# Routing attention and an ELU layer on one core: masking of three batches moved from TensorE to VectorE

## The chip, the cores and the metric

The kernel runs on one core of a Trainium2 chip. A core has five engines that work side by side, each through its own queue in order: TensorE (PE in the profile, its weight loads PEld), VectorE (DVE), ScalarE (ACT), GpSimd (POOL) and SyncE (SP), which issues the transfers. The metric is the device time of a run in microseconds.

## The reference

Inputs are q, k, v of shape (4, 8, 768, 64), that is batch, heads, sequence, head dimension; 16 centroids per head; and two weight matrices of 512x2048 and 2048x512.

```python
q_assign = argmax(q_n @ c_n.T)          # per head, 16 clusters; the same for k
mask = q_assign[:, :, :, None] == k_assign[:, :, None, :]
scores = where(mask, q @ k.T / 8, -1e9)
attn = softmax(scores)
x = (attn @ v)  ->  (3072, 512)         # heads side by side
h = x @ w_in
out = where(h > 0, h, exp(min(h, 0)) - 1) @ w_out
```

A query attends only to the keys of its own cluster. That mask is what the change is about.

## The kernel before

**Blocks.** Attention is done in 48 blocks: 4 batches x 3 thirds of the queries (256 each) x 4 pairs of heads. One block is one iteration n of the main loop. Scores are held transposed: keys on the 128 partitions, queries along the free dimension. A block has six key tiles; two of them with two heads make a unit of 128 x 1024 numbers, which fills one of three PSUM buffers called `banks` (two 2 KB banks each). So there are three units per block.

**The mask before.** `assign` makes a one-hot matrix `hot` (cluster by token, bf16): L370 finds the largest similarity, L374 compares with it, L384 transposes. Because a pair of heads must lie on either half of the partitions, a second copy with the halves swapped is made (L388 on ScalarE in batch 1, L390 on VectorE later). `masks` (L401, ScalarE, two instructions per block) turns the queries' part into `qm`, which is 0 for the token's own cluster and -2^80 for the others. In `scores`, `plain` (L425) multiplies queries and keys, a pair of matmuls of 64 rows each per key tile, and `mask` (L437) adds `hot` times `qm` into the same bank, again a pair. The exponential (L448, ScalarE) of a masked score is then exactly 0.

**Values.** `values(n)` multiplies the exponentials `p` with v into `o_bank` (L506) and sums them over the keys by a matmul with ones (L495) into a `banks` buffer. From block 10 on, VectorE first adds the three units (`sums`, L483 to L485), so that four matmul records instead of 24 are left of the row sums. ScalarE takes the logarithm of the sum (L524), copies it to `e` (L525; `e` shares its buffer with `sim`, which `assign` reads), copies `o_bank` (L526) and makes 1/sum (L527); L528 and L529 on VectorE refine it; L532 on GpSimd multiplies it into `xT`.

**The ELU layer.** For each third, with a lag of seven blocks, four groups of steps lie in the iterations, one group each:
- n mod 4 = 3: `hidden` 0 and 1. Each is 16 matmuls into one `banks` buffer (L547), then exp on ScalarE (L557), a clamp on GpSimd (L558) and, after the next hidden step was issued, `elu` on VectorE (L564, L566 or L568), which releases the buffer.
- n mod 4 = 0: `hidden` 2 and 3.
- n mod 4 = 1: products `first` to `fourth` (L577), into o_bank, f_bank, o_bank, f_bank in turn. ScalarE evicts o_bank (L608, L619), VectorE f_bank (L614, L624); between them VectorE adds operands for later products (L609, L615).
- n mod 4 = 2: products `fifth` to `seventh`, into f_bank, o_bank, f_bank. VectorE evicts (L630, L637, L645); GpSimd adds (L638, L639); two stores follow.

The seven products are a Strassen-like form of the second matmul.

**The order of an iteration** is written out by hand: `values(n-1)`, loads, `scores(n)`, `masks(n+1)`, `sums(n)`, then in the last four iterations of a batch two 32x32-block transposes of the next batch's q and k on VectorE (`turn`, L319), then the group of the ELU layer. In a batch's last iteration, between the two hidden steps and after them, stand the similarities of the next batch (`similar`: matmuls L353 in two halves, each into a `banks` buffer that VectorE's transpose L360 releases) and `assign`. The first nine iterations also unpack the weights on VectorE and ScalarE (L249 to L274) and add weights (L304 to L307, with L305 on GpSimd).

**The check.** Near the end `verdict` adds up evidence that the fast path was valid (L676 to L686 on VectorE), sums it over the partitions by a small matmul (L688) and writes a flag. A second path runs only if it fails.

Buffers of a pool are given out again in the order in which they were released; a matmul into a buffer waits until its last reader has finished.

Of the kernel before, what the change touches and what calls it, by code (L numbers as in the profile page):

```python
# [9 lines left out]
F32 = mybir.dt.float32  # L10
BF16 = mybir.dt.bfloat16
U32 = mybir.dt.uint32
I32 = mybir.dt.int32
Act = mybir.ActivationFunctionType
Alu = mybir.AluOpType
# [3 lines left out]
P = 128  # L19
# [41 lines left out]
def main_path(ctx, tc, c, q, k, v, centroids, moe_w_in, moe_w_out, out):  # L61
# [7 lines left out]
    NQ = 3  # L69
# [24 lines left out]
    def banks():  # L94
        return short.tile([P, 2, 512], F32, name="banks", tag="banks")
# [66 lines left out]
    for e in range(2):  # L162
        rows = slice(64 * e, 64 * e + 64)
        nc.vector.tensor_reduce(
            big[rows],
            ident[rows].rearrange("q (h x e c) -> q x e h c", h=2, x=2, e=2)[:, :, e],
            axis=Axis.XY,
            op=Alu.add,
        )
    minus = const.tile([P, 2], F32, name="minus")  # L170
    nc.vector.tensor_scalar(minus, big, -BIG, None, op0=Alu.mult)
    nc.vector.tensor_scalar(big, big, BIG, None, op0=Alu.mult)
# [22 lines left out]
    cT = const.tile([P, P], F32, name="cT")  # L195
    nc.vector.tensor_copy(cT, cps[:, :P])

    count = const.tile([P, 4 * B + 1], F32, name="count")
    counted = {}
    r_sum = const.tile([P, NQ * len(pairs)], F32, name="r_sum")  # L200
# [108 lines left out]

    T, sim, hot, qm = {}, {}, {}, {}
    name_of = "qk"

    def turn(i, j):
# [45 lines left out]

    def assign(b, j, at, size):
        if at == 0:
            hot[b, j] = route.tile([P, 2, S], BF16, name="hot", tag=f"hot{j}", bufs=1 + j)
        cols = slice(at, at + size)
        n = size // NC
        s = sim[b, j][:, cols].rearrange("p (n c) -> p n c", c=NC)
        top = route.tile([P, HS // NC], F32, name="top", tag="top", bufs=1)[:, :n]
        oh = route.tile([P, HS], BF16, name="oh", tag="oh", bufs=1)[:, :size]
        nc.vector.tensor_reduce(top, s, axis=Axis.X, op=Alu.max)  # L370
        at = counted.setdefault(size, [])
        at.append(len(at) + (0 if size == HS else 4 * B - 2))
        at = at[-1]
        nc.vector.scalar_tensor_tensor(  # L374
            oh.rearrange("p (n c) -> p n c", c=NC),
            s,
            1.0,
            top.unsqueeze(2).to_broadcast([P, n, NC]),
            op0=Alu.mult,
            op1=Alu.is_equal,  # L380
            accum_out=count[:, at : at + 1],
        )
        h = hot[b, j]
        nc.vector.transpose(h[:, 0, cols], oh)  # L384
        for e in range(2):
            at = 64 * e
            if b == 0:
                nc.scalar.copy(h[64 - at : 128 - at, 1, cols], h[at : at + 64, 0, cols])  # L388
            else:
                nc.vector.tensor_copy(h[64 - at : 128 - at, 1, cols], h[at : at + 64, 0, cols])  # L390

    def side(pr, e):
        return int(pr // 2 != e)

    def masks(n):
        b, third, pr = blocks[n]
        qm[n] = route.tile([P, QS], BF16, name="qm", tag="qm", bufs=2)
        for e in range(2):
            rows = slice(64 * e, 64 * e + 64)
            m = big[rows, pr % 2 : pr % 2 + 1]  # L400
            nc.scalar.activation(  # L401
                qm[n][rows],
                hot[b, 0][rows, side(pr, e), ts(third, QS)],
                Act.Identity,
                scale=m,
                bias=minus[rows, pr % 2 : pr % 2 + 1],
            )
# [9 lines left out]
    def scores(n):  # L417
        b, third, pr = blocks[n]
        i = b * NPR + pr
        cols = ts(third, QS)  # L420

        def plain(s, kt):
            for e in range(2):
                rows = slice(64 * e, 64 * e + 64)
                nc.tensor.matmul(  # L425
                    s[:, e, ts(kt % 2, QS)],
                    lhsT=T[i, 1][rows, ts(kt, P)],
                    rhs=T[i, 0][rows, cols],
                    start=n > 0 or kt % 2 == 0,
                    stop=False,  # L430
                    skip_group_check=n == 0,
                )

        def mask(s, kt):
            for e in range(2):
                rows = slice(64 * e, 64 * e + 64)
                nc.tensor.matmul(  # L437
                    s[:, e, ts(kt % 2, QS)],
                    lhsT=hot[b, 1][rows, side(pr, e), ts(kt, P)],
                    rhs=qm[n][rows],  # L440
                    start=False,
                    stop=True,
                    skip_group_check=n == 0,
                )

        def exponentials(s, u):
            p = pu[n, u] = probs.tile([P, 2, 2 * QS], F32, name="p", tag="p")
            nc.scalar.activation(p, s, Act.Exp, scale=SCALE)  # L448

        if n == 0:  # L450

            turn_first = similar(0, 1, 0, QS)
            turn_rest = similar(0, 1, QS, 2 * QS)
            units = [banks() for _ in range(2)]
            for u in range(2):
                for m in range(2):
                    plain(units[u], 2 * u + m)
            turn_first()
            for u in range(NT // 2):
                assign(0, 1, u * QS, QS)  # L460
                if u == 0:
                    turn_rest()
                if u == 1:
                    units.append(banks())
                    for m in range(2):
                        plain(units[2], 4 + m)
                for m in range(2):
                    mask(units[u], 2 * u + m)
                exponentials(units[u], u)
                weigh(1)  # L470
            return
        for u in range(NT // 2):
            s = banks()
            for m in range(2):
                plain(s, 2 * u + m)
                mask(s, 2 * u + m)
            exponentials(s, u)
            if n < LAG + 3:
                weigh(1)
# [105 lines left out]
    def outer(b, third):  # L585
# [4 lines left out]
        t1, t2, t4 = (w_sum[:, n] for n in range(3))  # L590
        seen = {}

        def temp():
            return loads.tile([P, 2, QS], F32, name="part", tag="ex", bufs=3)

# [30 lines left out]
            )  # L626

        def fifth():
            product(f_bank, g_sum, t2)
            nc.vector.tensor_tensor(  # L630
                seen["o"][1][:, :QS], f_bank[:, :QS], seen["ae"][:, 0], op=Alu.add
            )

        def sixth():
            product(o_bank, a_, t1)
            o, u4 = seen["o"][1], seen["dt"][:, 1]
            nc.vector.tensor_tensor(u4, o_bank[:, :QS], o[:, :QS], op=Alu.add)  # L637
            nc.gpsimd.tensor_tensor(o[:, :QS], o[:, :QS], seen["dt"][:, 0], op=Alu.add)  # L638
            nc.gpsimd.tensor_tensor(o[:, QS:], u4, seen["ae"][:, 1], op=Alu.add)  # L639
            store(1, o)  # L640

        def seventh():
            product(f_bank, b_, h_)
            o = seen["o"][0]
            nc.vector.tensor_tensor(o[:, QS:], f_bank[:, :QS], seen["dt"][:, 1], op=Alu.add)  # L645
            store(0, o)

        return [first, second, third_, fourth], [fifth, sixth, seventh]
# [19 lines left out]
            load("v", b * NPR + pr)  # L668
            raw["v", n] = raw.pop(("v", b * NPR + pr))

    def verdict():

        ok = c["ok"]
        peak = const.tile([P, 2], F32, name="peak")
# [9 lines left out]
            )  # L684
        nc.vector.tensor_reduce(ok[:, 2:3], same, axis=Axis.X, op=Alu.min)
        nc.vector.tensor_reduce(ok[:, 3:4], ok[:, 0:3], axis=Axis.X, op=Alu.min)  # L686
        ps = banks()[:, 0]
        nc.tensor.matmul(ps[:1, :1], lhsT=ok[:, 3:4], rhs=ones[:, :1], start=True, stop=True)  # L688
        nc.vector.tensor_copy(c["go"], ps[:1, :1])
# [14 lines left out]
    for n in range(len(blocks) + LAG):  # L704
# [18 lines left out]
        if n == 0:  # L723
            weigh(3)
        if n < len(blocks):
            if n >= LAG + 3:
                sums(n)
            if ahead and at in turns:
                for j in range(2):
                    turn((b + 1) * NPR + turns[at], j)  # L730
        beside = []
        if ahead and at + 1 == NB:
            beside.append(None)
            for j in range(2):
                beside.append(
                    lambda b=b, j=j: [similar(b + 1, j, half * HS, HS)() for half in range(2)]
                )
                beside.append(
                    lambda b=b, j=j: [assign(b + 1, j, half * HS, HS) for half in range(2)]
                )  # L740
            beside.append(lambda n=n: masks(n + 1))
        main = groups[n - LAG] if n >= LAG else []
        done = 0
        for m, step in enumerate(main):
            step()
            upto = len(beside) * (m + 1) // len(main)
            for other in beside[done:upto]:
                if other:
                    other()
            done = upto  # L750
            if n < LAG + 2:
                weigh(2 if n == LAG else 1)
# [3 lines left out]
        if n == LAG + 1:  # L756
            weigh(100)
            for half in range(2):
                sum_weights(half)
        if n == len(blocks) + 1:  # L760
            verdict()


# [252 lines left out]
```

## Time and profile before

| | |
|---|---|
| median of three runs | 1026.14 us (1025.75 to 1026.44) |
| profiled execution: time, span | 1026.78 us, 1024.7 us |
| TensorE busy | 1001.1 us, 6331 records |
| VectorE busy | 474.8 us, 771 records |
| ScalarE busy | 354.1 us, 609 records |
| GpSimd busy | 112.5 us, 129 records |
| granted TensorE clock | 0.998 |

An fp32 matmul shows as two records, so 12 score matmuls are 24. Records of matmuls overlap: the mean duration of one (0.38 us at 256 columns) is more than the distance from one to the next, and what a matmul costs is read from the distance. In a line of the groups the columns are: line, engine, operation, output <- inputs, shapes, count | busy us, mean ns | idle time before, and what ended it. In a line of the timeline: start and length in us, engine, line, operation, count, and in brackets idle time before.

### The profile page before, as it was taken

Reading aid. Unit: us, or ns where it says so; the run is one execution under the profiler, and the core shown is the slowest. Engines: PE = TensorE matmul, PEld = TensorE weight load, DVE = VectorE, ACT = ScalarE, POOL = GpSimd, SP = SyncE. Lnnn points to the kernel's source line nnn. Section 1 sums busy time; section 2 is a strip of 40 time slices with the busy share of each in tenths; the row PEclk is TensorE's granted clock in tenths of the full one; section 3 lists DMA queues with packets and bytes.
Section 4 is the critical chain, followed back from the end, with each engine's and each line's share of the span. In section 5 each row is a group of like instructions: output and inputs, shape, how many; then the busy total and the mean of one; then the engine's idle time right before and its main releaser. Section 6 shows DMA issues by size and latency. Waiting matters only on the chain.

```text
span 1024.7 us, 15010 instructions
## 1 busy us (share of the span) xinstructions
PE 1001.1 (98%) x6331; PEld 778.4 (76%) x6331; DVE 474.8 (46%) x771; ACT 354.1 (35%) x609; POOL 112.5 (11%) x129
## 2 busy tenths in 40 slices
PE   6999999999999999999999999999999999999997
PEld 4567777778778877777778778768877877888886
DVE  7999972753244244473334344375224324423131
ACT  6787422342243234232432333233234223321010
POOL 0010130110110110110110111011011011011010
PEclk9999999999999999999999999999999999999999
DMA  8857222100132122100122104100011011000000
GB/s 281 316 165 197 54 43 59 27 21 16 37 69 39 36 48 62 36 17 16 52 47 48 52 20 72 53 17 16 16 39 30 16 36 32 16 21 1 21 1 24
DMA packets 103962, 55.60 MB, mean 54 GB/s; under 512 B 83408, under 2 KB 96720, under 8 KB 103888
## 3 DMA queue, kind: packets, MB, share of 16 engines
q1 hardware_dynamic: 103888, 54.57, 19.3%
q8 instruction: 52, 0.85, 0.3%
q14 instruction: 22, 0.18, 0.0%
HBM read 48.27 MB, written 6.29 MB: 53 GB/s over the span
## 4 chain that ended last, share of the span: by engine, by line
PE 81%; DVE 12%; ACT 3%; issue 2%; DMA 1%; POOL 0%; SPq 0%; DVEq 0%; POOLq 0%; ACTq 0%
PE banks L547 30%; PE f_bank L577 16%; PE o_bank L577 12%; PE o_bank L506 10%; PE banks L425 9%; PE banks L437 2%; PE banks L495 2%; DVE ex L249 2%; DVE w_in L252 1%; DVE w_in L255 1%; DVE w_out L252 1%; ACT p L448 1%; DVE ex L271 1%; PE banks L353 1%; DVE w_out L255 1%
## 5 line engine op out<-in xcount | busy, mean ns | idle before, releaser
L547 PE MATMUL banks<-xT,w_in 128*128 128x256 f32 x1536 | 338.3, 381 | 0.8 <-ACT p L448 0.3
L547 PEld LDWEIGHTS banks<-xT,w_in 128*128 128x128 f32 x1536 | 289.8, 190 | 48.5 <-issue 3.6
L425 PE MATMUL banks<-qT,kT 64*128 64x256 f32 x1152 | 166.0, 388 | 3.3 <-ACT p L448 1.2
L557 ACT ACTIVATE gT<-banks 128x1024 f32<-128x1024 f32 x48 | 49.2, 1024 | 283.5 <-PE banks L547 283.5
L506 PE MATMUL o_bank<-p,v_raw 128*64 128x256 f32 x1152 | 144.7, 386 | 2.2 <-ACT p L448 1.9
L448 ACT ACTIVATE p<-banks 128x1024 f32<-128x1024 f32 x144 | 144.5, 1020 | 6.4 <-PE banks L437 4.2
L564 DVE SCALAR_TENSOR_TENSOR gT<-gT,banks 128x1024 f32<-128x1024 f32 x48 | 58.4, 1217 | 163.3 <-POOL gT L558 163.2
L425 PEld LDWEIGHTS banks<-qT,kT 64*128 64x128 f32 x1152 | 88.0, 187 | 53.0 <-PE o_bank L506 10.0
L506 PEld LDWEIGHTS o_bank<-p,v_raw 128*64 128x64 f32 x1152 | 78.4, 137 | 56.0 <-issue 15.2
L524 ACT ACTIVATE r<-banks 128x256 f32<-128x256 f32 x48 | 18.4, 384 | 232.9 <-PE banks L495 232.9
L558 POOL TENSOR_SCALAR gT<-gT 128x1024 f32<-128x1024 f32 x48 | 50.7, 1056 | 346.0 <-ACT gT L557 346.0
L577 PE MATMUL o_bank<-w_out,gT 128*128 128x256 f32 x384 | 87.8, 382 | 0.0
L528 DVE TENSOR_TENSOR e<-e,r 128x256 f32<-128x256 f32 x48 | 20.4, 424 | 145.4 <-ACT r L527 145.2
L577 PE MATMUL f_bank<-w_out,gT 128*128 128x256 f32 x384 | 86.8, 379 | 0.0
L532 POOL TENSOR_TENSOR xT<-xT,r 128x256 f32<-128x256 f32 x48 | 37.4, 779 | 435.5 <-DVE r L529 380.8
L437 PE MATMUL banks<-qm,hot 64*128 64x256 bf16 x576 | 79.7, 269 | 2.7 <-ACT hot L388 1.6
L577 PEld LDWEIGHTS o_bank<-w_out,gT 128*128 128x128 f32 x384 | 72.1, 190 | 12.6 <-issue 3.2
L577 PEld LDWEIGHTS f_bank<-w_out,gT 128*128 128x128 f32 x384 | 73.0, 190 | 9.9
L483 DVE TENSOR_TENSOR psum<-p 128x1024 f32<-128x1024 f32 x38 | 46.6, 1226 | 36.1 <-ACT p L448 36.1
L401 ACT ACTIVATE qm<-hot,minus,big 64x256 bf16<-64x256 bf16 x96 | 56.7, 591 | 1.0
L484 DVE TENSOR_TENSOR psum<-psum,p 128x1024 f32<-128x1024 f32 x38 | 46.6, 1225 | 6.0 <-ACT p L448 2.6
L577 PE MATMUL f_bank<-w_sum,g_sum 128*128 128x256 f32 x192 | 44.6, 386 | 0.6 <-DVE part L624 0.6
(111 smaller groups left out, 808.1 us busy)
## 6 DMA issues: line engine op xcount, KB each, us to landing
v_raw<-in_v_dram SPq DMA_DIRECT2D x48, 384.0 KB, 3.2
w_sum<-in_moe_w_out_dram SPq DMA_DIRECT2D x12, 512.0 KB, 5.1
out_dram<-o_sb SPq DMA_DIRECT2D x24, 256.0 KB, 2.0
q_raw<-in_q_dram SPq DMA_DIRECT2D x48, 96.0 KB, 3.1
k_raw<-in_k_dram SPq DMA_DIRECT2D x48, 96.0 KB, 2.9
w_sum<-in_moe_w_in_dram SPq DMA_DIRECT2D x8, 512.0 KB, 8.4
w_out<-in_moe_w_in_dram SPq DMA_DIRECT2D x8, 512.0 KB, 10.7
w_out<-in_moe_w_out_dram SPq DMA_DIRECT2D x4, 512.0 KB, 4.1
```

The costliest lines, as they stand in the source:

```text
L401: nc.scalar.activation(qm[n][rows], hot[b, 0][rows, side(pr, e), ts(third, QS)], Act.Identity, scale=m, bias=minus[rows, pr % 2 : pr % 2 + 1],
L425: nc.tensor.matmul(s[:, e, ts(kt % 2, QS)], lhsT=T[i, 1][rows, ts(kt, P)], rhs=T[i, 0][rows, cols], start=n > 0 or kt % 2 == 0, stop=False ...
L437: nc.tensor.matmul(s[:, e, ts(kt % 2, QS)], lhsT=hot[b, 1][rows, side(pr, e), ts(kt, P)], rhs=qm[n][rows], start=False, stop=True, skip_gr ...
L448: nc.scalar.activation(p, s, Act.Exp, scale=SCALE)
L483: nc.vector.tensor_tensor(to, pu[n, 0], pu[n, 1], op=Alu.add)
L484: nc.vector.tensor_tensor(to, to, pu[n, 2], op=Alu.add)
L506: nc.tensor.matmul(o_bank[64 * e : 64 * e + 64, :QS], lhsT=raw["v", n][:, e, kt], rhs=p[:, e, ts(m, QS)], start=(kt == 0), stop=(kt == NT ...
L547: nc.tensor.matmul(hf[:, f], lhsT=w_in[:, ch, ts(4 * n + f, P)], rhs=xT[b, third][:, ch], start=(ch == 0 and f % 2 == 0), stop=(ch == KC - 1),
L557: nc.scalar.activation(t, hf, Act.Exp)
L558: nc.gpsimd.tensor_scalar(t, t, 1.0, 0.0, op0=Alu.min, op1=Alu.max)
L564: nc.vector.scalar_tensor_tensor(t, t, -1.0, hf, op0=Alu.add, op1=Alu.max)
L577: nc.tensor.matmul(to[:, :QS], lhsT=left[:, f], rhs=right[:, f], start=(f == 0), stop=(f == FC // 2 - 1),)
```

## The change

Batch 1 stays as it was. In batches 2 to 4:

- `scores` leaves the mask matmuls out, and `masks` does nothing. The swapped copy of `hot` is not made.
- `key_numbers`, once a batch: six matmuls of `hot` (keys) with `index`, a 128x8 table, give each key's cluster number per head; ScalarE copies them to `kc`.
- `query_numbers`, once a third: eight matmuls of 32 rows spread the queries' cluster numbers over all partitions, in two lots of four into f_bank and o_bank (one time a `banks` buffer); ScalarE copies them to `qc` as bytes. They stand in the iterations with n mod 4 = 0, which use neither bank for products.
- `keep_same`, once a block: twelve VectorE instructions of 128x256 multiply `p` by (query's number == key's number), in place, the key's number being a scalar per partition.
- `sums` starts at block 9 instead of 10 and stands after `turn` and `keep_same`; in iterations with three products it stands after the second of them.
- `verdict` is split: the VectorE part in iteration 49 and the matmul in 50.
- In the last two thirds `fifth` and `seventh` use o_bank and `sixth` f_bank.
- `index` is made at the start: 16 memsets on GpSimd, three instructions on VectorE.

```diff
+    numbers = const.tile([P, NC], F32, name="numbers")
+    for n in range(NC):
+        nc.gpsimd.memset(numbers[:, n : n + 1], float(n))
+    index = const.tile([P, H], BF16, name="index")
...
+    wide_index = work.tile([P, H, NC], F32, name="wide_index", tag="r", bufs=1)
+    nc.vector.tensor_tensor(
+        wide_index,
+        ident.rearrange("q (h c) -> q h c", c=NC),
+        numbers.unsqueeze(1).to_broadcast([P, H, NC]),
+        op=Alu.mult,
+    )
+    sums_of = const.tile([P, H], F32, name="sums_of")
+    nc.vector.tensor_reduce(sums_of, wide_index, axis=Axis.X, op=Alu.add)
+    nc.vector.tensor_copy(index, sums_of)
...
-        for e in range(2):
+        for e in range(2 if b == 0 else 0):
             at = 64 * e
-            if b == 0:
-                nc.scalar.copy(h[64 - at : 128 - at, 1, cols], h[at : at + 64, 0, cols])
-            else:
-                nc.vector.tensor_copy(h[64 - at : 128 - at, 1, cols], h[at : at + 64, 0, cols])
+            nc.scalar.copy(h[64 - at : 128 - at, 1, cols], h[at : at + 64, 0, cols])
...
+    def key_numbers(b):
+        ps = banks()[:, 0]
+        kc[b] = route.tile([P, NT, H], F32, name="kc", tag="kc", bufs=2)
+        for kt in range(NT):
+            nc.tensor.matmul(
+                ps[:, ts(kt, H)], lhsT=hot[b, 1][:, 0, ts(kt, P)], rhs=index, start=True, stop=True
+            )
+        nc.scalar.copy(kc[b].rearrange("p t h -> p (t h)"), ps[:, : NT * H])
+
+    def query_numbers(b, third, places):
+        if (b, third) not in qc:
+            qc[b, third] = route.tile([P, H, QS], U8, name="qc", tag="qc", bufs=1)
+        for e in range(2):
+            for pr, ps in places:
+                rows = slice(32 * pr, 32 * pr + 32)
+                nc.tensor.matmul(
+                    ps[:, ts(e, QS)],
+                    lhsT=index[rows, 2 * pr + e : 2 * pr + e + 1].to_broadcast([32, P]),
+                    rhs=hot[b, 0][rows, 0, ts(third, QS)],
+                    start=True,
+                    stop=True,
+                )
+        for pr, ps in places:
+            nc.scalar.copy(
+                qc[b, third][:, 2 * pr : 2 * pr + 2], ps.rearrange("p (e n) -> p e n", e=2)
+            )
+
+    def keep_same(n):
+        b, third, pr = blocks[n]
+        for u in range(NT // 2):
+            for e in range(2):
+                for m in range(2):
+                    p = pu[n, u][:, e, ts(m, QS)]
+                    nc.vector.scalar_tensor_tensor(
+                        p,
+                        qc[b, third][:, 2 * pr + e],
+                        kc[b][:, 2 * u + m, 2 * pr + e : 2 * pr + e + 1],
+                        p,
+                        op0=Alu.is_equal,
+                        op1=Alu.mult,
+                    )
...
             for m in range(2):
                 plain(s, 2 * u + m)
-                mask(s, 2 * u + m)
+                if b == 0:
+                    mask(s, 2 * u + m)
...
+        turn_on = (b * NQ + third) * 4 + 3 + LAG > len(blocks)
+        fifth_bank, sixth_bank = (o_bank, f_bank) if turn_on else (f_bank, o_bank)
...
         if n < len(blocks):
-            if n >= LAG + 3:
-                sums(n)
             if ahead and at in turns:
                 for j in range(2):
                     turn((b + 1) * NPR + turns[at], j)
...
         main = groups[n - LAG] if n >= LAG else []
+        extra = {}
+        if n < len(blocks):
+            late = [lambda n=n: sums(n)] if n >= LAG + 2 else []
+            if b > 0:
+                third = at // NPR
+                q_in = lambda b, third, places: (lambda: query_numbers(b, third, places))
+                if at == 0:
+                    extra[0] = [
+                        lambda b=b: key_numbers(b),
+                        q_in(b, third, [(0, f_bank), (1, o_bank)]),
+                        lambda n=n: keep_same(n),
+                    ] + late
+                    extra[1] = [
+                        lambda b=b, third=third: query_numbers(
+                            b, third, [(2, f_bank), (3, banks()[:, 0])]
+                        )
+                    ]
+                else:
+                    if at % NPR == 0:
+                        query_numbers(b, third, [(0, f_bank), (1, o_bank)])
+                        extra[0] = [q_in(b, third, [(2, f_bank), (3, o_bank)])]
+                    keep_same(n)
+                    if len(main) == 3 and at % NPR == 2:
+                        extra[1] = late
+                    else:
+                        late and late[0]()
+            else:
+                late and late[0]()
         done = 0
         for m, step in enumerate(main):
             step()
+            for other in extra.get(m, []):
+                other()
```

More of the change, by code (lines that the diff above doesn't have):

```diff
@@ L12 @@
 U32 = mybir.dt.uint32
+U8 = mybir.dt.uint8
 I32 = mybir.dt.int32
@@ L307, in sum_weights @@
         nc.vector.tensor_tensor(t4, g_, t2, op=Alu.subtract)
-    T, sim, hot, qm = {}, {}, {}, {}
+    T, sim, hot, qm, qc, kc = {}, {}, {}, {}, {}, {}
     name_of = "qk"
@@ L363, in assign @@
         if at == 0:
-            hot[b, j] = route.tile([P, 2, S], BF16, name="hot", tag=f"hot{j}", bufs=1 + j)
+            hot[b, j] = route.tile(
+                [P, 2 if b == 0 else 1, S], BF16, name="hot", tag=f"hot{j}", bufs=1
+            )
         cols = slice(at, at + size)
@@ L384, in assign @@
         nc.vector.transpose(h[:, 0, cols], oh)
-        for e in range(2):
+        for e in range(2 if b == 0 else 0):
             at = 64 * e
-            if b == 0:
-                nc.scalar.copy(h[64 - at : 128 - at, 1, cols], h[at : at + 64, 0, cols])
-            else:
-                nc.vector.tensor_copy(h[64 - at : 128 - at, 1, cols], h[at : at + 64, 0, cols])
+            nc.scalar.copy(h[64 - at : 128 - at, 1, cols], h[at : at + 64, 0, cols])
     def side(pr, e):
         return int(pr // 2 != e)
+    def key_numbers(b):
[37 more added lines that the diff above has]
+                    )
     def masks(n):
         b, third, pr = blocks[n]
+        if b > 0:
+            return
         qm[n] = route.tile([P, QS], BF16, name="qm", tag="qm", bufs=2)
@@ L429, in plain @@
                     start=n > 0 or kt % 2 == 0,
-                    stop=False,
+                    stop=b > 0,
                     skip_group_check=n == 0,
@@ L628, in fifth @@
         def fifth():
-            product(f_bank, g_sum, t2)
+            product(fifth_bank, g_sum, t2)
             nc.vector.tensor_tensor(
-                seen["o"][1][:, :QS], f_bank[:, :QS], seen["ae"][:, 0], op=Alu.add
+                seen["o"][1][:, :QS], fifth_bank[:, :QS], seen["ae"][:, 0], op=Alu.add
             )
         def sixth():
-            product(o_bank, a_, t1)
+            product(sixth_bank, a_, t1)
             o, u4 = seen["o"][1], seen["dt"][:, 1]
-            nc.vector.tensor_tensor(u4, o_bank[:, :QS], o[:, :QS], op=Alu.add)
+            nc.vector.tensor_tensor(u4, sixth_bank[:, :QS], o[:, :QS], op=Alu.add)
             nc.gpsimd.tensor_tensor(o[:, :QS], o[:, :QS], seen["dt"][:, 0], op=Alu.add)
@@ L642, in seventh @@
         def seventh():
-            product(f_bank, b_, h_)
+            product(fifth_bank, b_, h_)
             o = seen["o"][0]
-            nc.vector.tensor_tensor(o[:, QS:], f_bank[:, :QS], seen["dt"][:, 1], op=Alu.add)
+            nc.vector.tensor_tensor(o[:, QS:], fifth_bank[:, :QS], seen["dt"][:, 1], op=Alu.add)
             store(0, o)
@@ L669, in load_v, with findings @@
             raw["v", n] = raw.pop(("v", b * NPR + pr))
-    def verdict():
+    def findings():
         ok = c["ok"]
@@ L686, in verdict @@
         nc.vector.tensor_reduce(ok[:, 3:4], ok[:, 0:3], axis=Axis.X, op=Alu.min)
+    def verdict():
+        ok = c["ok"]
         ps = banks()[:, 0]
@@ L740, in main_path @@
                 )
-            beside.append(lambda n=n: masks(n + 1))
         main = groups[n - LAG] if n >= LAG else []
+        extra = {}
+        if n < len(blocks):
+            late = [lambda n=n: sums(n)] if n >= LAG + 2 else []
+            if b > 0:
+                third = at // NPR
[9 more added lines that the diff above has]
+                            b, third, [(2, f_bank), (3, banks()[:, 0])]
+                        )
+                    ]
[10 more added lines that the diff above has]
+                late and late[0]()
         done = 0
@@ L760, in main_path @@
         if n == len(blocks) + 1:
+            findings()
+        if n == len(blocks) + 2:
             verdict()
```

## The prediction

> **What bounds the kernel now.** I read the busy table and the costliest groups first, then TensorE's waits, then the timeline of one block.
>
> ```profile
> PE 1001.1 (98%) x6331; PEld 778.4 (76%) x6331; DVE 474.8 (46%) x771; ACT 354.1 (35%) x609; POOL 112.5 (11%) x129
> L448 ACT ACTIVATE p<-banks 128x1024 f32<-128x1024 f32 x144 | 144.5, 1020 | 6.4 <-PE banks L437 4.2
> L437 PE MATMUL banks<-qm,hot 64*128 64x256 bf16 x576 | 79.7, 269 | 2.7 <-ACT hot L388 1.6
> L528 DVE TENSOR_TENSOR e<-e,r 128x256 f32<-128x256 f32 x48 | 20.4, 424 | 145.4 <-ACT r L527 145.2
> ```
>
> TensorE is busy 98% of the span, so work taken from it shortens the span, and anything that makes it wait lengthens it. VectorE is busy 46%. The masks' 79.7 us is not what they cost: matmuls overlap. The timeline of one block (iteration 26) prices them:
>
> ```profile
> 487.38 0.70 PE L425 MATMUL banks<-qT,kT 64*128 64x256 f32 x4
> ...
> 487.92 0.28 PE L437 MATMUL banks<-qm,hot 64*128 64x256 bf16 x2
> ...
> 488.03 0.60 PE L425 MATMUL banks<-qT,kT 64*128 64x256 f32 x4
> ...
> 488.46 0.28 PE L437 MATMUL banks<-qm,hot 64*128 64x256 bf16 x2
> ...
> 488.57 0.60 PE L425 MATMUL banks<-qT,kT 64*128 64x256 f32 x4
> ...
> 488.91 3.07 ACT L448 ACTIVATE p<-banks 128x1024 f32<-128x1024 f32 x3
> ...
> 490.84 3.72 PE L577 MATMUL f_bank<-w_sum,g_sum 128*128 128x256 f32 x16
> ```
>
> Another stretch of the timeline, in the first block:
>
> ```profile
> 19.83 2.00 PE L425 MATMUL banks<-qT,kT 64*128 64x256 f32 x16
> ```
>
> With a mask pair between them, score pairs follow each other by 0.54 us (488.03 to 488.57). The line of the first block has four pairs without masks, 16 records: 2.00 us less one duration of 0.38 over 15 steps is 0.108 per record, 0.43 per pair. A mask pair therefore costs 0.54 - 0.43 = **0.11 us** of TensorE.
>
> I count from t, the start of a block's first score matmul. In this block the scores last 490.84 - 487.38 = 3.46 us, and the first exponential ends at 488.91 + 1.02 - 487.38 = t+2.55, the others 1.02 apart.
>
> [...]L271 begins 0.34 us after L263 (28.29 and 28.63 in the VectorE timeline), though each lasts 0.42. [...]L307 takes 3.26 us while GpSimd's L305 runs; its like, L306, takes 1.22. [...]a mask pair of 0.27 us records costs 0.11.
>
> **The change, part by part**, names and lines of the kernel before. The iterations of a third differ in what follows the block's scores: hidden 0 and 1 (n mod 4 = 3), hidden 2 and 3 (0), four products (1), three products (2).
>
> *Masks off TensorE.* 36 blocks x 6 pairs x 0.11 = 24 us at most. A block's scores go from 3.46 to 24 x 0.108 + 0.2 = 2.78 us: 0.68 less, where the banks allow it. Score unit 2 takes the bank of the row sums, free when L525 has read it (t+1.05), and it is wanted at t+1.8: no wait. Hidden 0 takes the bank of unit 0, free at t+2.55, wanted at t+2.78: just no wait. So the 27 blocks with n mod 4 of 1, 2, 3 gain 27 x 0.68 = **-18.4 us**. With n mod 4 = 0 one bank is still held by hidden 1, and unit 2 waits for the first exponential. Before, it began at 527.81 - 525.21 = t+2.60; it can't be earlier now. There the scores go from 3.88 to 3.46.
>
> *Cluster numbers.* Per third eight matmuls of 32 rows by 256, in two lots of four; per batch six of 128x8. No row shows them. From the mask pair (two halves of the array at once, 0.11) I take 0.22 for a lot of four; not overlapped it would be 0.43. The six small ones: 0.45 in all by the 0.094 of L437's weight load[...]. Six blocks (n mod 4 = 0, not first in a batch): -0.42 + 2 x 0.3 with a change-over each, 0.17 x 6 = **+1.0**. Three first blocks: the trace has 4.40 us there (202.83 to 207.23), with a 0.27 wait for `e`, whose buffer VectorE's L374 still reads. That wait should go, the two copies of L390 having left the queue; scores 3.46, so -0.94 + 0.45 + 0.5 = 0, and 0.3 for a late bank: **+0.9** in all. ScalarE gains four 0.6 us evictions a third (between L526's 0.37 for 256 columns and L326's 0.81 for 768) and loses L401's 1.2 us per block: no one waits longer for it.
>
> *Masking on VectorE.* 432 instructions, twelve per block, in place between exponential and values. Three unknowns: a byte input, a pointer scalar, two SBUF inputs. Below, [...]L263/L271 show 0.34 for instructions of 0.42. Above, fully serial is L528's 0.424 + 0.03. The two L192 (64 columns, pointer scalar) take 0.42 together, 0.25 alone: 0.17, or 0.10 over the columns' 0.067. For 256: 0.267 + 0.10 = **0.37**. Twelve: 4.45, and 0.5 for the collision with L532 on GpSimd (L252 slowed from 0.69 to 1.21 that way at 116.80). It starts at t+2.57 (first exponential, L529) and ends at t+7.5. What is queued behind:
> - Three sums (L483 to L485), 3.2 us: t+10.7.
> - Four-product iterations: L609 (1.2) and L614 (0.42): t+12.3. L614 releases f_bank to the fourth product, due at 2.78 + 3 x 3.45 = t+13.15. Covered by 0.8; the transposes L319 (1.86 us, ahead of the masking in two such iterations of batches 2 and 3) use the cover up: 2 x 0.6 = **+1.2**.
> - Three-product iterations: L630 comes before the sums and is done at t+7.9, needed at t+9.7; the sums end, with L638 and L639 colliding, near t+14.5, needed at t+15.7. Nothing.
> - First-hidden iterations: only ELU is behind; its bank is wanted at t+19. But at a batch's end (two of them) L319 and the similarities share the queue: masking ends at t+9.2, sums at t+12.4, the transpose L360 at t+13, and hidden 1 waits for the bank that it reads from t+11.2. L360 used to wait 2.9 us for TensorE instead. 2 x 1.6 = **+3**.
> - The values read p from t+13 at the earliest: covered by 5 us. In a batch's first block masking starts late (t+12.6, behind hidden 2 and two evictions), ends at t+17.5, and values start at t+18.6.
>
> *Sums one block earlier* (n = 9). Row sums drop from 24 to 4 records: 161.79 - 156.46 = 5.33 against 3.17, -2.16. But VectorE, behind the weight sums, does L614 at 152.34, where the fourth product already waits 0.24; 3.2 us of sums now lie ahead of it: +3.3. **+1.1.**
>
> *Tail.* The check's matmul no longer stands where it waits 1.54 us for L686, and the fifth product changes bank (0.59 at 1008.81): **-2.1**. *Head.* 16 memsets on GpSimd and three small VectorE instructions fit where VectorE idles 1.98 us (ended at 8.07): 0, up to +0.8 if not. DMAs are not moved past any queue.
>
> Sum: -18.4 + 1.0 + 0.9 + 1.2 + 3.0 + 1.1 - 2.1 = **-13.3 us**. The profiled execution has span 1024.7 and time 1026.78, 0.6 above the median of 1026.14. Subtracted from the median: 1012.8, said as 1013.
>
> **Rivals.** *VectorE becomes the bound* (slower). If the twelve instructions have pitch p, L614 ends at t + 2.57 + 0.5 + 12p + 3.2 + 1.6 = t + 7.9 + 12p, and is late from p = 0.44. Beyond, every 0.01 costs 0.12 us in nine four-product, three first and two last blocks of batches: 1.7 us. The gain is gone at p = 0.52; at 0.60 it is 1026.1 - 13.3 + 27 = 1040. For it: no row has a byte input beside a pointer; GpSimd's collisions fall in this queue. Against it: fully serial is 0.45, and GpSimd is busy 11%.
>
> *Banks eat the gain.* The exponentials take 3.07 us per block against scores of 2.78. If hidden 0 or unit 2 gets the later of two banks, it waits about 0.8 us; in nine first-hidden iterations the 0.68 is gone: 1013 + 6 = 1019; with the lots of four unoverlapped (+4) 1023. For it: the margin is 0.23 us. Against it: the bank freed longest ago is the next to be taken.
>
> *Everything covered.* No wait at the batches' ends or at n = 9: 1013 - 5 = 1008, and 1005 without the cost of cluster numbers.
>
> **How the numbers follow.** As forecast or better, 1005 to 1017: 0.58. Banks, 1017 to 1024: 0.20. VectorE late: 0.22, of which 0.05 land within 0.2% (2.05 us, about what a measurement of this kernel can tell from no change) and 0.17 beyond, up to 1040. Faster 0.78, same 0.05, slower 0.17. Range 1005 to 1028: it leaves out the slow rival and little below.
>
> **What would show it.** Right: scores of 2.8 us; 432 VectorE records 0.35 to 0.40 us apart; VectorE near 640 us busy; a wait of hidden 1 for L360's successor in two iterations and a longer one of the fourth product at n = 9. Wrong: waits of products on VectorE in every third, values waiting for the masking, or scores that wait for exponentials in three kinds of iteration of four.

## The result and the profile after

The changed kernel takes **1022.46 us** (1021.67 to 1022.95, four runs) against 1026.27 us: a ratio of 0.9963, 95% interval 0.9946 to 0.998. It is faster by 3.8 us, where 13.3 us were forecast: the sign was right, the size was not. Its profiled span is 1020.9 us, 3.8 less than before. The four runs took 1022.87, 1022.06, 1021.67 and 1022.95 us at granted clocks of 0.990, 0.992, 0.994 and 0.990; the first of them is the profiled one, whose timeline is read below.

Lines of the page after; the columns are those of the page before:

```profile
PE 990.2 (97%) x5969; PEld 773.0 (76%) x5969; DVE 661.9 (65%) x1185; ACT 324.5 (32%) x576; POOL 135.5 (13%) x145
L449 DVE SCALAR_TENSOR_TENSOR p<-qc,kc,p 128x256 f32<-128x256 uint8 x432 | 184.8, 499 | 37.7 <-ACT qc L438 37.6
```

TensorE is busy 11 us less, but the span fell by 3.8. The block of iteration 26 looks as forecast:

```profile
489.81 2.86 PE L490 MATMUL banks<-qT,kT 64*128 64x256 f32 x24
...
492.26 5.31 DVE L449 SCALAR_TENSOR_TENSOR p<-qc,kc,p 128x256 f32<-128x256 uint8 x12
492.46 0.87 POOL L598 TENSOR_TENSOR xT<-xT,r 128x256 f32<-128x256 f32 x1 [18.44 <-DVE r L595]
...
492.60 3.72 PE L643 MATMUL f_bank<-w_sum,g_sum 128*128 128x256 f32 x16
```

Scores last 492.60 - 489.81 = 2.79 us (2.78 forecast). The twelve masking instructions take 5.31 us while GpSimd runs beside the first two, 4.80 us where it doesn't (iterations 23 and 35): a pitch (time from one start to the next) of 0.40 us (0.37 forecast) and 0.5 for the collision.

So the loss lies elsewhere. To find it I took the start of every block's scores in both timelines and looked at how their difference changes from block to block (us; minus is faster):

| iterations | forecast, each | measured, each | measured, sum |
|---|---|---|---|
| 23 undisturbed ones of batches 2 to 4 with n mod 4 = 1, 2, 3 | -0.68 | -0.67; -0.54 in 13, 25, 37 | -15.0 |
| 21, 33 (four products, with `turn`) | -0.08 | -0.27 | -0.54 |
| 16, 20, 28, 32, 40, 44 (hidden 2 and 3) | +0.17 | +0.51 | +3.04 |
| 12, 24, 36 (first block of a batch) | +0.3 | +1.05 | +3.15 |
| 23, 35 (last block, with masking) | +0.8 | +2.90, +3.25 | +6.15 |
| 9 (sums one block earlier) | +1.1 | +2.5 | +2.5 |
| tail after block 47's scores, its own -0.67 (in row 1) apart | -2.1 | -2.4 | -2.4 |

Together -3.1; another -0.7 was there before iteration 9, which gives the -3.8 of the span. That -0.7 is not put down to the change: the two dose kernels below, whose head is the old one, start the fourth product of iteration 9 0.68 and 0.95 us earlier than the profile of before.

Where TensorE waited, after (who waited for whom: us in total, times, longest):

```profile
PE banks L613 <- DVE sim L376: 4.3, 2, 2.3
PE f_bank L643 <- DVE o_sb L683: 3.4, 1, 3.4
...
PE banks L490 <- DVE gT L630: 1.2, 3, 0.4
```

The first and second line are waits that the prediction had (3 and 3.5 us). But iteration 23 lost 2.90 + 0.67 = 3.57 us with a wait of only 1.97. TensorE's timeline there, and then its granted clock, in stretches of the length of the slow one (columns: stretch, its length, PE busy, records in brackets, clock, DMA share, GB/s):

```profile
430.21 1.50 PE L369 MATMUL banks<-qT,cT 128*32 128x384 f32 x16
433.68 8.86 PE L613 MATMUL banks<-xT,w_in 128*128 128x256 f32 x32 [1.97 <-DVE sim L376]
```
```profile
431.37:434.79 3.42, 1.45 (x12) 1.00 0.00 0
434.79:438.20 3.41, 3.41 (x10) 0.50 0.00 0
438.20:441.61 3.41, 3.41 (x17) 1.00 0.00 0
```

Hidden 1 takes 8.86 us for 32 records; elsewhere it takes 7.17. The wait was followed by 3.41 us in which TensorE was granted half of its clock; that alone costs 1.7 us. The fourth product of iteration 9 shows the same after its 3.43 us: it lasts 5.20 us, against 3.72 in the kernel before (first line).

```profile
152.81 3.72 PE L577 MATMUL f_bank<-w_sum,gT 128*128 128x256 f32 x16 [0.24 <-DVE o_sb L614]
```
```profile
155.27 5.20 PE L643 MATMUL f_bank<-w_sum,gT 128*128 128x256 f32 x16 [3.43 <-DVE o_sb L683]
```
```profile
151.47:154.89 3.42, 0.37 (x2) 1.00 0.86 136
154.89:158.30 3.41, 3.03 (x7) 0.50 0.52 82
```

The wait of 2.32 us in iteration 35 has such a stretch as well:

```profile
677.12:680.53 3.41, 3.41 (x10) 0.50 0.00 0
```

In the kernel before, the granted clock was 1.00 from 31.10 to 1024.30 us. In the changed kernel a stretch of 3.41 us at half clock began from 0.38 us before to 1.11 us after the end of each of these three waits. That the wait is the cause is what the expectations below call the clock theory; the experiments test it.

### The profile page after: what moved, and what is told of

The parts are those of the page before. It is cut to its first block, busy times and chain, and to the rows that moved or that the text cites. A ratio compares the mean times of both kernels' runs of the same rounds, so it can differ in the third digit from the quotient of the medians.

```text
span 1020.9 us, 14717 instructions
## 1 busy us (share of the span) xinstructions
PE 990.2 (97%) x5969; PEld 773.0 (76%) x5969; DVE 661.9 (65%) x1185; ACT 324.5 (32%) x576; POOL 135.5 (13%) x145
## 4 chain that ended last, share of the span: by engine, by line
PE 74%; DVE 17%; ACT 4%; issue 3%; DMA 1%; POOL 0%; DVEq 0%; ACTq 0%; POOLq 0%
PE banks L613 27%; PE f_bank L643 15%; PE o_bank L643 11%; PE o_bank L572 10%; PE banks L490 8%; DVE p L449 3%; DVE ex L265 2%; PE banks L561 1%; ACT p L513 1%; DVE w_in L268 1%; DVE w_out L268 1%; DVE w_in L271 1%; DVE psum L550 1%; DVE ex L287 1%; DVE psum L549 1%
## 5 line engine op out<-in xcount | busy, mean ns | idle before, releaser
L613 PE MATMUL banks<-xT,w_in 128*128 128x256 f32 x1536 | 344.2, 384 | 5.0 <-DVE sim L376 4.3
L449 DVE SCALAR_TENSOR_TENSOR p<-qc,kc,p 128x256 f32<-128x256 uint8 x432 | 184.8, 499 | 37.7 <-ACT qc L438 37.6
L490 PE MATMUL banks<-qT,kT 64*128 64x256 f32 x1152 | 147.8, 389 | 5.6 <-ACT p L513 4.5
L490 PEld LDWEIGHTS banks<-qT,kT 64*128 64x128 f32 x1152 | 101.1, 186 | 45.2 <-PE o_bank L572 10.0
L630 DVE SCALAR_TENSOR_TENSOR gT<-gT,banks 128x1024 f32<-128x1024 f32 x48 | 58.2, 1213 | 68.4 <-POOL gT L624 68.3
L624 POOL TENSOR_SCALAR gT<-gT 128x1024 f32<-128x1024 f32 x48 | 53.0, 1104 | 351.6 <-ACT gT L623 325.7
L643 PE MATMUL o_bank<-w_out,gT 128*128 128x256 f32 x416 | 95.1, 382 | 0.0
L643 PEld LDWEIGHTS o_bank<-w_out,gT 128*128 128x128 f32 x416 | 78.2, 190 | 13.5 <-ACT p L513 2.0
L643 PE MATMUL f_bank<-w_out,gT 128*128 128x256 f32 x352 | 79.6, 379 | 0.0
L643 PEld LDWEIGHTS f_bank<-w_out,gT 128*128 128x128 f32 x352 | 66.9, 190 | 9.1
L643 PE MATMUL f_bank<-w_sum,gT 128*128 128x256 f32 x224 | 52.4, 388 | 3.7 <-DVE o_sb L683 3.4
L643 PEld LDWEIGHTS f_bank<-w_sum,gT 128*128 128x128 f32 x224 | 43.4, 195 | 10.9 <-DVE o_sb L683 4.9
## 6 DMA issues: line engine op xcount, KB each, us to landing
w_out<-in_moe_w_in_dram SPq DMA_DIRECT2D x8, 512.0 KB, 10.5
```

What stands on the lines that cost most here:

```text
L449: nc.vector.scalar_tensor_tensor(p, qc[b, third][:, 2 * pr + e], kc[b][:, 2 * u + m, 2 * pr + e : 2 * pr + e + 1], p, op0=Alu.is_equal, op ...
L490: nc.tensor.matmul(s[:, e, ts(kt % 2, QS)], lhsT=T[i, 1][rows, ts(kt, P)], rhs=T[i, 0][rows, cols], start=n > 0 or kt % 2 == 0, stop=b > 0 ...
L613: nc.tensor.matmul(hf[:, f], lhsT=w_in[:, ch, ts(4 * n + f, P)], rhs=xT[b, third][:, ch], start=(ch == 0 and f % 2 == 0), stop=(ch == KC - 1),
L624: nc.gpsimd.tensor_scalar(t, t, 1.0, 0.0, op0=Alu.min, op1=Alu.max)
L630: nc.vector.scalar_tensor_tensor(t, t, -1.0, hf, op0=Alu.add, op1=Alu.max)
L643: nc.tensor.matmul(to[:, :QS], lhsT=left[:, f], rhs=right[:, f], start=(f == 0), stop=(f == FC // 2 - 1),)
```

## The experiments

**e1_sums10.** Sums from block 10 on:

```diff
-            late = [lambda n=n: sums(n)] if n >= LAG + 2 else []
+            late = [lambda n=n: sums(n)] if n >= LAG + 3 else []
```

> Sums from block 10 on, as before; all else as changed. Clock theory[...]: the wait of 3.43 us before the fourth product of iteration 9 goes back to about 0.2 and its 5.20 us to 3.62; the row sums of block 9 cost their 2.16 us again; net 2.5 us faster than the changed kernel, some 1020.0. Rival (the slow fourth product has another cause, such as the weights being in use by VectorE and GpSimd at that time): it stays near 5.2 us without the wait, and the gain is only 1 us.

Measured: 1018.32 us, 4.1 less than the changed kernel. The difference to before stays at -0.83 through iteration 9: the 2.5 us are gone. The rest came unexpected and says more. Iteration 23 lost 1.21 us instead of 2.90, with the same wait and the same work:

```profile
431.06 7.17 PE L613 MATMUL banks<-xT,w_in 128*128 128x256 f32 x32 [1.97 <-DVE sim L376]
```
```profile
426.43:429.84 3.41, 2.66 (x22) 1.00 0.00 0
429.84:433.26 3.42, 2.20 (x10) 1.00 0.00 0
```

A wait of 1.97 us with the granted clock at 1.00 around it, and no slow matmuls after it: length alone doesn't decide. Iteration 35 of the same run, after a wait of 2.2 us, still lost 3.15.

**e2_end_late.** In the last iterations of batches 2 and 3 the sums come after hidden 1:

```diff
-                    if len(main) == 3 and at % NPR == 2:
+                    if len(main) == 3 and at % NPR == 2 or ahead and at + 1 == NB:
                         extra[1] = late
```

> In the last iterations of batches 2 and 3 the sums stand after the second hidden step, so that VectorE's transposes of the similarities come ahead of them; all else as changed. Clock theory: no wait of hidden 1, its 32 records take 7.2 us instead of 8.9, and iterations 23 and 35 last 0.67 us less than before the change instead of 2.90 and 3.25 us more: 7.5 us faster than the changed kernel, some 1015.0. Rival (the slow hidden 1 has a cause of its own): the wait of 2.0 and 2.3 us goes, but hidden 1 stays near 8.9 us: 4.3 us faster, some 1018.

Measured: 1016.64 us, 5.8 less. Iterations 23 and 35 now gain 0.67 us each, hidden 1 takes 7.17. That is 7.5 us in these two. It gave back 0.6 us in each of 24 and 36 (+1.64 instead of +1.05), where ScalarE waits for the buffer of `e`, and 1.4 us at iteration 9, which the edit doesn't touch: there the fourth product took 6.59 us instead of 5.20 after the same wait, with the granted clock at 0.50 for two stretches of 3.41 us instead of one.

**e3_fill.** Four matmuls with an unused result in the place of the wait, VectorE untouched:

```diff
+        def fill():
+            for _ in range(4):
+                nc.tensor.matmul(
+                    f_bank[:, :QS], lhsT=w_in[:, 0, :P], rhs=w_in[:, 1, :QS], start=True, stop=True
+                )
...
                     lambda b=b, j=j: [similar(b + 1, j, half * HS, HS)() for half in range(2)]
+                    + ([fill()] if b > 0 and j == 0 else [])
```

> As changed, with four matmuls of 128x256 (8 records, 1.7 us, their result unused) in the place where TensorE waits for VectorE in iterations 23 and 35. VectorE's order and lateness are untouched. Clock theory: hidden 1 still can't start earlier, but its 32 records take 7.2 us instead of 8.9: 2 x 1.7 = 3.4 us faster than the changed kernel, some 1019. Rival (VectorE's lateness, or what it does meanwhile, slows hidden 1): the records stay at 8.9 us and the time is that of the changed kernel, 1022.5.

Measured: 1019.91 us, 2.6 less. Hidden 1 starts no earlier, as VectorE is as late as before. Iteration 35, in the changed kernel (first line) and here:

```profile
676.50 8.86 PE L613 MATMUL banks<-xT,w_in 128*128 128x256 f32 x32 [2.32 <-DVE sim L376]
```
```profile
672.46 2.00 PE L805 MATMUL f_bank<-w_in 128*128 128x256 f32 x8
674.84 7.17 PE L613 MATMUL banks<-xT,w_in 128*128 128x256 f32 x32 [0.39 <-DVE sim L376]
```
```profile
671.56:674.97 3.41, 3.02 (x22) 1.00 0.00 0
674.97:678.38 3.41, 3.41 (x16) 1.00 0.02 5
```

Adding useless work to TensorE made the kernel faster: the clock stayed at 1.00 where it had been 0.50 for 3.41 us. Iterations 23 and 35 went from +2.90 and +3.25 to +1.22 and +1.56, that is 1.69 us each. Iteration 35 shows the clock, and with it the wait, to be the cause, not what VectorE does meanwhile. Iteration 23 shows less: in e1 hidden 1 kept its 7.17 us there without any filling.

**e4_no_keep.** The loop of `keep_same` runs over no units:

```diff
-        for u in range(NT // 2):
+        for u in range(0):
```

> As changed, without the twelve masking instructions of each block on VectorE: batches 2 to 4 are not masked. What is left is TensorE's part and the cluster numbers. If VectorE's lateness is what took the gain: the waits at iterations 23 and 35 (7.5 us with the slow clock), in iterations 12, 24, 36 (some 0.8 each) and 20, 32 (0.4 each) go, the wait at iteration 9 stays: 10 us faster than the changed kernel, some 1012. If the score gain itself were smaller than thought, or the cluster numbers cost the rest: within 2 us of the changed kernel.

Measured: 1011.93 us, 10.5 less. The waits at 23 and 35 and in 21 and 33 are gone, iterations 12, 24, 36 lose 0.20 instead of 1.05; 16, 20 and their like still lose 0.50. (Iteration 9 lost 3.91 us here, with two stretches at half clock, as in e2.) So VectorE's lateness took 0.85 us in each first block, and what remains there and in the hidden 2 and 3 iterations is left to the cluster numbers, which e6 takes out.

**e6_const.** The cluster numbers are set once and never computed:

```diff
+    nc.gpsimd.memset(same_q, 1)
+    nc.gpsimd.memset(same_k, 1.0)
...
     def key_numbers(b):
+        return
...
     def query_numbers(b, third, places):
+        return
...
-                        qc[b, third][:, 2 * pr + e],
-                        kc[b][:, 2 * u + m, 2 * pr + e : 2 * pr + e + 1],
+                        same_q[:, 2 * pr + e],
+                        same_k[:, 2 * u + m, 2 * pr + e : 2 * pr + e + 1],
...
-                            b, third, [(2, f_bank), (3, banks()[:, 0])]
+                            b, third, [(2, f_bank), (3, f_bank)]
```

With this a batch's first block also takes two `banks` buffers fewer, so what it gains is not the price of the matmuls alone.

> As changed, with the numbers of queries and keys set once to the same constant: no matmuls and evictions for them, VectorE's masking instructions all there (nothing is masked in batches 2 to 4). Price of the cluster numbers on TensorE: the first lot costs 0.32 us and the second, which breaks the hidden steps' stream, 0.53: iterations 16, 20, 28, 32, 40, 44 should go from +0.50 to -0.34, so 5 us together, and the three first blocks of batches lose their 1.2 us of matmuls and, since masking starts earlier, their 0.85 us of waits: 6 us. In all 11 us faster than the changed kernel, some 1011.5. If the lots overlap with the rest and only VectorE counts, it is within 3 us of the changed kernel.

Measured: 1011.56 us, 10.9 less. Hidden 2 and 3 iterations go from +0.50 to -0.34, that is 0.84 us for two lots of four; first blocks from +1.05 to -0.78. In the changed kernel's timeline the lots themselves are short, but the fp32 stream is broken around them:

```profile
529.84 0.28 PE L430 MATMUL f_bank<-hot,index 32*128 32x256 bf16 x1
...
530.16 7.17 PE L613 MATMUL banks<-xT,w_in 128*128 128x256 f32 x32
...
537.27 0.28 PE L430 MATMUL f_bank<-hot,index 32*128 32x256 bf16 x1
...
537.59 7.17 PE L613 MATMUL banks<-xT,w_in 128*128 128x256 f32 x32
```

The same hidden steps in e6:

```profile
523.97 14.08 PE L619 MATMUL banks<-xT,w_in 128*128 128x256 f32 x64
537.98 2.38 PE L578 MATMUL o_bank<-p,v_raw 128*64 128x256 f32 x20
```

From a lot's start to hidden's start it is 0.32 us. Hidden 2 alone lasts 537.27 - 530.16 = 7.11 us and hidden 3 lasts 7.10, together 0.2 more than the 537.98 - 523.97 = 14.01 that both take without a break. So the second lot, which makes the break, costs 0.52 and the first 0.32.

**e5_dose and e5b_dose.** The kernel before, with more and more VectorE work ahead of L614's counterpart, so that the fourth product waits:

```diff
             o0, _ = seen["o"] = out_tile(), out_tile()
+            T_ = b * NQ + third
+            for _ in range(15 + T_ if 0 < T_ < 10 else 0):
+                nc.vector.tensor_tensor(
+                    o0[:, QS:], w_in[:, 0, :QS], w_in[:, 1, :QS], op=Alu.add
+                )
```

e5b_dose has `26 - T_`.

> The kernel before, with 16 to 24 additions of 128x256 on VectorE ahead of the eviction L614 in thirds 1 to 9 (one more in each third; their result is overwritten later). The fourth product then waits 0.4 to 3.2 us. Clock theory: short waits cost only themselves and the product takes 3.62 to 3.72 us; from some length on it takes up to 1.7 us longer, at a granted clock near 0.5 to 0.7 for 3.4 us. If the lowered clock came from anything but the wait, no product would take longer.

> As e5_dose with the order turned round, 25 additions in third 1 down to 17 in third 9, so that each length of wait falls at another moment. If the length alone decides, the threshold is the same as in e5_dose[...].

Each is one execution, read for its products and not for its time. The waits came out longer than meant (2.0 to 6.4 us). Two products of e5_dose:

```profile
239.79 5.41 PE L577 MATMUL f_bank<-w_sum,gT 128*128 128x256 f32 x16 [1.96 <-DVE o_sb L619]
```
```profile
323.79 3.72 PE L577 MATMUL f_bank<-w_sum,gT 128*128 128x256 f32 x16 [2.52 <-DVE o_sb L619]
```

The granted clock in the first 3.4 us of each:

```profile
239.80:243.20 3.40, 3.40 (x10) 0.61 0.02 5
323.80:327.20 3.40, 3.40 (x16) 1.00 0.03 7
```

All 20 products of the two dose kernels, two of them without added work:

| wait, us | products | length of the product, us |
|---|---|---|
| 0.23 | 2 | 3.72 |
| 1.96 | 1 | 5.41 |
| 2.43, 2.52, 2.88 | 3 | 3.72 |
| 3.34 to 4.71 | 7 | 5.19 to 5.41 |
| 5.02 to 6.40 | 7 | 6.36 to 6.71 |

So the lowered clock comes with the wait: the same product of the same kernel takes longer after a long wait only. But the length of the wait doesn't settle it: after 1.96 us it was slow, after 2.52 us in the same run and 2.43 and 2.88 in the other it wasn't. Against 3.72 us a product paid 1.5 to 1.7 us after waits of up to 4.71 us, where it paid at all, and 2.6 to 3.0 after those of 5.02 us and more.

A wait of 3.44 us passed without it, too. In e6 iteration 9 has it; the granted clock was 1.00 from 151.21 to 158.04 us, the fourth product takes 3.72 us, and the iteration loses 1.03 instead of 2.51:

```profile
156.47 3.72 PE L649 MATMUL f_bank<-w_sum,gT 128*128 128x256 f32 x16 [3.44 <-DVE o_sb L689]
```
```profile
151.21:154.62 3.41, 1.83 (x9) 1.00 0.56 89
154.62:158.04 3.42, 1.57 (x7) 1.00 0.89 139
```

Of the eight waits of 1.96 to 2.88 us told here (four dosed ones, two in the changed kernel, two in e1) four were followed by slow matmuls.

**e7_best.** e1, and the ends of batches with the first addition of the sums ahead of the transposes and the other two after hidden 1, and a batch's first block with its numbers earlier:

```diff
+                    elif ahead and at + 1 == NB:
+                        sums_first(n)
+                        extra[1] = [lambda n=n: sums_rest(n)]
...
-                    extra[0] = [
-                        lambda b=b: key_numbers(b),
-                        q_in(b, third, [(0, f_bank), (1, o_bank)]),
-                        lambda n=n: keep_same(n),
-                    ] + late
...
+                    key_numbers(b)
+                    query_numbers(b, third, [(0, f_bank)])
+                    extra[0] = [q_in(b, third, [(1, f_bank), (2, o_bank)])]
+                    extra[1] = [q_in(b, third, [(3, f_bank)])]
+                    keep_same(n)
+                    late[0]()
```

`key_numbers` writes to o_bank here instead of a `banks` buffer.

> Sums from block 10 on; in the last iterations of batches 2 and 3 the first addition of the sums ahead of the similarities' transposes and the other two after the second hidden step; in a batch's first block the cluster numbers of the keys and of the first pair are made ahead of hidden 2 (in o_bank and f_bank), those of pairs 2 and 3 after it and those of pair 4 after hidden 3. If the four mended waits add up (2.5 at iteration 9, 7.4 at 23 and 35, and the 0.85 by which VectorE is late in iterations 12, 24, 36, less 0.3 for another change-over each): 11 us faster than the changed kernel, some 1011.5. Rival (a mended wait comes back in another place, as with the 0.6 us that e2 lost to the buffer of e): 1013 to 1016.

Measured: **1010.75 us**, ratio to the kernel before 0.9853 (0.9836 to 0.9869): 15.4 us, four times the gain of the change. Iterations 23 and 35 gain 0.67 us, 24 and 36 lose 0.53; VectorE is as busy as in the changed kernel (657.9 us):

```profile
428.02 1.20 DVE L376 STREAM_TRANSPOSE sim<-banks 128x384 f32<-128x384 f32 x2 [0.73 <-PE banks L369]
428.66 7.17 PE L620 MATMUL banks<-xT,w_in 128*128 128x256 f32 x32
```

VectorE waits for TensorE again at the transposes, not the other way round.

## Why the prediction was right or wrong

- **Masks off TensorE: right.** 0.67 us a block, and the bank margins held: without the masking on VectorE all 27 blocks keep it (e4). The hidden 2 and 3 iterations kept the score gain at -0.34 (e6) against -0.42.
- **Masking on VectorE: right in kind.** Pitch 0.40 instead of 0.37 us. The sum of columns and pointer came close; L263 and L271, whose 0.34 stood beside it, have 512 columns and one input and say little of it. The 0.267 for 256 columns does agree with the record before: 0.69 us for 512 (L252) less 0.42 for 256 (L528). The masking is covered in all ordinary blocks, and the fourth product doesn't wait in ordinary thirds. The rival, VectorE as the bound, didn't come.
- **The step that failed: the waits at a batch's end and at iteration 9 were priced at their own length.** The prediction found all three (+3 and +1.1) and had the lengths nearly right: 1.97 and 2.32 us where 1.6 was worked out, 3.43 where 3.5. It let TensorE go on at full speed afterwards: the granted clock, 0.998 over the span before, has no term in its sum. The lowered clock added 1.69, 1.69 and 1.48 us, together 4.9 of the 9.5 us that are missing. All three have 3.41 us at a clock of 0.50 beside them in the trace; filling the wait (e3) took that away in iteration 35, and in other runs it was missing after a wait of the same length in 23 (1.97 us, e1) and 9 (3.44 us, e6). That all three were hit in the profiled execution is in part chance: the clocks of the four runs, 0.990 to 0.994, show that they lost different amounts.
- **Mis-sized: cluster numbers.** A lot was put at 0.3 us with its change-over. It costs 0.32 where a stream ends anyway and 0.52 in the middle of hidden steps; with the smaller score gain, six iterations lost 0.51 instead of 0.17 each: 2 us.
- **Mis-sized: first blocks of batches.** 0.3 us each for a late bank; VectorE's lateness took 0.85 (e4): the row sums wait 0.18 us for the sums and the next scores 0.39 for ELU's release (L630) behind them; the other 0.28 was not traced to a wait. Here GpSimd's collisions count: L551 took 1.41 us beside L624 on GpSimd instead of 0.69. With the lots' own excess +1.05 instead of +0.3: 2.2 us.
- The remaining 0.3 us is a balance: longer waits at 23 and 35 (1.1 together, 0.2 of it from 2 x 1.6 being put down as 3) and a smaller gain in the undisturbed blocks (0.6, of which 0.4 in 13, 25 and 37) against better values in 21 and 33 (0.4), in the tail (0.3) and the -0.7 of the head. **Tail and sums** as such were right: -2.4 for -2.1, and iteration 9 loses 1.03 where the clock stays up (e6; +1.1 forecast).
- The prediction's own view "Everything covered" (1008) was a better goal than it seemed: e7 gets to 1010.75 by order alone.

## What to carry to other kernels

A wait of a TensorE that is otherwise always busy can cost more than its length. Here it took another 1.5 to 1.7 us after four of the eight waits of 1.96 to 2.88 us, and 1.5 to 3.0 us after all 14 dosed waits of 3.34 us and more, though not after one of 3.44 us in another run (e6). Price such a wait above its length, as a range, or fill it with matmuls (e3). When work moves to an engine with much idle time, look for the few places where another step of that engine releases a buffer (here a batch's end), and put the moved work behind that step; the average load says nothing about them. A lot of four small bf16 matmuls cost 0.52 us inside an fp32 stream and 0.32 where the stream ends anyway.

## What the runs showed of the hardware

- In the changed kernel TensorE's granted clock was 0.50 for 3.41 us at each of the waits of 1.97, 2.32 and 3.43 us, from 0.38 us before to 1.11 us after the wait's end on, and the matmuls there took 8.86 us instead of 7.17 (twice) and 5.20 instead of 3.72. In the kernel before, without these waits, it was 1.00 from 31.10 to 1024.30 us.
- A wait of 1.97 us was followed by the lower clock in one run and not in another (the changed kernel, e1), and one of 3.44 us wasn't (e6). Nor was a stretch of 2.3 us that had been filled with matmuls (e3, iteration 35: 1.00 from 671.56 to 678.38 us).
- In the dose kernels a product of 3.72 us took 5.19 to 5.41 us after the seven waits of 3.34 to 4.71 us and 6.36 to 6.71 after the seven of 5.02 to 6.40.
- A masking instruction (128x256, byte input, pointer scalar, two inputs from SBUF) has a pitch of 0.40 us, and its record lasts 0.44 to 0.49 us, and 0.48 to 0.96 where GpSimd runs beside it.
